# Half of one block's reciprocal loads on ScalarE's queue, two more tiles transposed by DMA, and a new order, in a linear-attention and feed-forward kernel

## The chip, the cores and the metric

The kernel runs on one core of a Trainium2 chip. The metric is the time of one execution on the device, in microseconds (us). The five engines of the core work side by side: TensorE (PE, matmuls; PEld its weight loads), VectorE (DVE), ScalarE (ACT), GpSimd (POOL) and SyncE (SP). Each works through its own instructions in order and waits on semaphores for the others. Transfers are issued by an engine's queue (here SP's, and after the change ScalarE's too) and carried out by DMA engines.

## The reference

A transformer block on 2048 tokens of width 512, in bf16: linear attention with 32 heads of 16, then a feed-forward part of width 1792, each behind a layer norm and with a residual.

```python
x = A_x
h = x + _A_ref(_layernorm(x), A_wqkv, A_wo)
h2 = h + _B_ref(_layernorm(h), B_w1, B_w2)
# _A_ref, on x = layernorm of the input
q, k, v = heads of x @ wqkv
phi = lambda t: jnp.where(t > 0, t + 1, jnp.exp(t)) + 1e-6
pq, pk = phi(q), phi(k)
kv = jnp.einsum("bhsd,bhse->bhde", pk, v)
z = jnp.einsum("bhsd->bhd", pk)
num = jnp.einsum("bhqd,bhde->bhqe", pq, kv)
den = jnp.einsum("bhqd,bhd->bhq", pq, z)[..., None] + 1e-6
return (num / den, heads joined) @ wo
# _B_ref
return maximum(x @ w1, 0) @ w2
```

## The kernel before

The tokens are 16 tiles of 128, in four blocks (c = 0 to 3) of 512. All work is written as words in one list, ORDER (line 18); the loop at line 555 emits them one after the other, and each word is a small function `op_...`. A word such as `K.1.0.0.2` is the function's name and its numbers. The words of one engine run in the order of the list; between engines only the semaphores of true dependences count. So ORDER fixes five queues, and nothing else sets the order. PSUM is one tile `bk` of eight banks, and the last number or so of a word on TensorE is its bank; a word that writes a bank waits until the bank's last reader is done.

The stages, with their words:

- Loads on SP: `lx` (x, in groups of tiles), `lk`, `lq`, `lv`, `lo`, `l1`, `l2` (weights for k, q, v, wo, w1, w2; the last two in halves of 896 KB).
- First layer norm, tile t: `S` (statistics, VectorE), `A` (their sum, VectorE), `R` (inverse root, two instructions on ScalarE), `N` (normalise into `h_nat`, VectorE). Then the transpose into `lnT[c]`: tiles 0 to 4 on TensorE (`T`, four 128x128 transposes against an identity, with the eviction `E` on ScalarE), tiles 5 to 15 by a DMA transpose on SP (`X`, line 308).
- Keys, tile t: `K` (four matmuls of 512 columns, or two halves of two), `F` (exp) and `U` (relu) on ScalarE out of PSUM, `M` (min with 1) and `D` (add) on VectorE into pk. Queries, block c, quarter j: `Q` and likewise `qF`, `qU`, `qM`, `qD` into `pqT[c]`.
- The statistics product `G` of tile t: four matmuls of ln by pk into banks 4 to 7, summed over all 16 tiles (G multiplies by what `D` of the tile wrote). The sums z: `za`, `zf`, `zhi`, `zlo` on VectorE and the short matmuls `z`; `zc`, `zh` on VectorE.
- `gA`, `gD` evict G (ScalarE, VectorE); `kv` multiplies by the v weights, `kx` (VectorE) masks to the heads' blocks, `m` multiplies by wo, `mA` and `mD` evict that.
- The denominators of block c: `d4` (TensorE), `dl4` and `dx4` (ScalarE, ln and exp(-)), `wb` (a store of the reciprocals to a scratch tensor in DRAM, SP), `rb` (line 470: eight loads from it, one for each head position, each spread over 16 partitions of `rr`), `dm` (VectorE: pqT by rr into `pqs`; two instructions of two quarters each). There is one `rr`, so the loads of a block wait for the `dm` of the block before.
- Tile t: `h` (pqs by m, TensorE), `hD` (plus x, VectorE), second norm `s`, `a`, `r`, `n` or `nA` (VectorE or ScalarE), whose transpose is `t` (TensorE, four transposes) with the copy `v` (VectorE), or `x` (DMA transpose on SP, line 309). Tiles 2 and 3 have `t` and `v`, all others `x`.
- Feed-forward: `p` (w1, 512 tokens) or `ph` (256 of them: half 0 is tiles 0 and 1 of the block, half 1 is tiles 2 and 3), evicted in pairs by `pD` (VectorE) or `pA` (ScalarE) with the relu; `f` (w2, tile t, the fourteen slices f in two halves of seven), `fo` (VectorE, scale and residual), `fd` (store, SP).
- `warm` are matmuls on zeros at the start, `masks` and `const` constants.

Two functions of TensorE matter for the change: `op_K` (line 312) and `op_f` (line 533) set start at slice 0 and stop at the last slice, so their halves run in rising order.

Of the kernel before, what the change touches and what calls it, by code (L numbers as in the profile page):

```python
# [34 lines left out]
ph.0.1.3.0 ph.0.2.0.0 ph.0.3.1.1 qM.2.2.2 qM.3.0.2 ph.0.0.2.0 ph.0.0.2.1 qM.3.2.2 qD.3.0.2 qU.3.2.2 qD.2.2.2  # L35
ph.0.2.0.1 qD.3.2.2 p.0.7.5 d4.2.6.2 pD.0.2.2 dl4.2 dl4.3 rb.1.4 rb.1.6 rb.1.3 rb.1.2 rb.1.0 rb.1.1 ph.0.1.3.1
rb.1.7 rb.1.5 p.0.6.4 dx4.2 dm.1.0.2 dm.1.2.2 h.4.0 pD.0.0.2 hD.4 pD.0.6.2 p.0.5.1 h.6.6 dx4.3 p.0.4.0 hD.6
l2.7.7 h.5.4 pA.0.4.2 s.4 s.6 hD.5 h.7.7 a.4 a.6 p.0.11.6 p.0.10.5 s.5 hD.7 a.5 p.0.9.4 wb.2 rb.2.6 n.4 rb.2.0
rb.2.4 s.7 n.6 rb.2.3 rb.2.2 rb.2.1 a.7 n.5 n.7 rb.2.5 rb.2.7 dm.2.0.2 dm.2.2.2 pD.0.10.2 p.0.13.1 p.0.12.0
p.0.8.3 pD.0.12.2 wb.3 r.4.4 rb.3.0 rb.3.4 h.10.7 hD.10 x.6 h.8.2 h.11.6 hD.8 s.10 rb.3.5 rb.3.1 rb.3.6  # L40
f.1.0.0.7 rb.3.3 rb.3.2 rb.3.7 s.8 hD.11 pD.0.8.2 h.9.5 f.3.1.0.7 x.7 x.5 s.11 a.8 hD.9 f.1.0.7.7 f.0.4.0.7 a.10
a.11 x.4 dm.3.2.2 dm.3.0.2 h.14.7 h.12.3 s.9 n.11 h.15.6 a.9 n.10 h.13.2 fo.1 n.9 n.8 hD.14 s.14 hD.12 x.11
hD.15 f.0.4.7.7 r.8.4 p.1.13.7 p.1.6.3 a.14 hD.13 s.12 s.15 s.13 a.12 a.15 a.13 n.14 p.1.12.6 n.13 f.3.1.7.7
n.12 n.15 p.1.2.5 fo.0 pD.1.12.2 x.10 p.1.7.4 fo.3 p.1.3.6 x.9 pD.1.6.2 pD.1.2.2 r.12.4 x.8 p.1.11.2 p.1.10.1
pD.1.10.2 f.2.4.0.7 p.2.0.6 p.2.1.7 f.2.4.7.7 pD.2.0.2 p.2.10.0 p.2.11.1 fo.2 x.14 p.2.6.2 p.2.7.3 x.15 fd.3
p.2.13.7 p.2.12.6 pD.2.10.2 pD.2.6.2 x.12 fd.1 pD.2.12.2 p.2.2.0 x.13 fd.0 p.2.3.1 p.1.5.6 p.1.4.5 pD.2.2.2
pD.1.4.2 p.1.0.3 p.1.1.4 p.1.9.1 p.1.8.0 pD.1.0.2 pD.1.8.2 f.4.4.0.7 f.4.4.7.7 fo.4 fd.4 f.5.3.0.7 f.5.3.7.7
fo.5 fd.2 f.6.7.0.7 f.6.7.7.7 fo.6 p.2.4.2 p.2.5.3 f.7.0.0.7 f.7.0.7.7 pD.2.4.2 fo.7 p.3.6.1 p.3.7.2 pD.3.6.2
# [539 lines left out]
```

## Time and profile before

| | us |
|---|---|
| median of 3 runs | 169.78 |
| lowest and highest | 169.41, 170.17 |
| span of the profiled execution | 168.0 |

The profiled execution's time outside its span is not in the records; the difference of median and span is 1.78 us. The profile's page gives each engine's busy time and share of the span, and the span in 40 slices of 4.2 us with the busy tenths of each engine. The chain of waits goes back from the last instruction to what released it each time. The timeline lists instructions in order of time, like ones merged (x2 are two); its columns are start, length, engine, line, operation, written and read tile, shapes. TensorE's ends are modelled: matmuls overlap, so a single one shows as 0.38 us long.

The memory side: the 16 DMA engines are busy in tenths `4984054681595364414552520000101000011021` over the 40 slices.

### The profile page before, as it was taken

The page shows a single profiled execution, that of the slowest core. Times are in us where ns is not written, and L with a number is a line of the kernel's source. Part 1 is how long each engine was busy: PE and PEld are TensorE (multiplying, and loading weights), DVE is VectorE, ACT ScalarE, POOL GpSimd, SP SyncE. Part 2 cuts the span into 40 slices and gives each one's busy share as a digit, 9 for nine tenths or more (in the row PEclk, how much of TensorE's full clock was granted, in tenths as well). Part 3 has the DMA queues.
Part 4 walks back from the last instruction along what each step waited for, and adds up shares of the span by engine and source line. Part 5 has one row for each costly group of instructions (what it writes and reads, how often), then busy time and mean ns, then how long its engine had stood idle before and what let it go on. Part 6 is the DMA issues. An engine that isn't in the chain of part 4 may idle for free.

```text
span 168.0 us, 2417 instructions
## 1 busy us (share of the span) xinstructions
PE 162.7 (97%) x924; PEld 79.2 (47%) x924; DVE 115.6 (69%) x217; ACT 49.5 (29%) x83; POOL 4.8 (3%) x21
## 2 busy tenths in 40 slices
PE   7799999999999999999999999999999999999992
...
DVE  3899999942579999999999755764144773432312
...
DMA  4984054681595364414552520000101000011021
GB/s 108 353 298 88 20 106 95 189 301 45 132 337 161 98 205 132 132 48 123 83 102 57 126 63 0 0 0 0 62 31 35 0 0 7 32 34 48 31 94 39
DMA packets 25003, 16.01 MB, mean 95 GB/s; under 512 B 15008, under 2 KB 23968, under 8 KB 24992
## 3 DMA queue, kind: packets, MB, share of 16 engines
...
q8 instruction: 7, 0.11, 0.3%
...
## 4 chain that ended last, share of the span: by engine, by line
PE 92%; DMA 4%; SPq 2%; DVE 1%; issue 0%
PE bk L537 28%; PE bk L508 27%; PE bk L324 8%; PE bk L368 8%; PE bk L493 8%; PE bk L316 7%; DMA wq_sb<-in_A_wqkv_dram 4%; PE bk L517 2%; SPq L214 2%; PE bk L440 1%; DVE gT L545 1%; PE bk L392 1%; PE bk L414 1%; PE bk L426 1%; PE bk L287 0%
## 5 line engine op out<-in xcount | busy, mean ns | idle before, releaser
L537 PE MATMUL bk<-w_sb,at 128*128 128x512 bf16 (+2 forms) x252 | 50.0, 355 | 0.0
L508 PE MATMUL bk<-lnT,w_sb 128*128 128x512 bf16 x208 | 46.9, 379 | 0.0
L528 DVE TENSOR_SCALAR at<-bk 128x1024 bf16<-128x1024 f32 x27 | 32.8, 1223 | 13.2 <-PE bk L508 13.2
L537 PEld LDWEIGHTS <-at 128*128 128x128 bf16 x252 | 23.5, 98 | 25.4
L508 PEld LDWEIGHTS <-w_sb 128*128 128x128 bf16 x208 | 20.4, 98 | 23.9
L545 DVE SCALAR_TENSOR_TENSOR gT<-bk,rstd,h_nat 128x512 bf16<-128x512 f32 (+2 forms) x18 | 12.4, 691 | 24.6 <-PE bk L537 22.0
L334 ACT ACTIVATE eb<-bk 128x1024 bf16<-128x1024 f32 (+1 forms) x18 | 16.6, 929 | 5.3 <-PE bk L316 2.8
L337 ACT ACTIVATE rb<-bk 128x1024 bf16<-128x1024 f32 (+1 forms) x18 | 16.4, 929 | 0.0
L324 PE MATMUL bk<-lnT,wq_sb 128*128 128x512 bf16 x64 | 15.1, 379 | 0.3 <-DMA wq_sb<-in_A_wqkv_dram 0.3
L316 PE MATMUL bk<-wk_sb,lnT 128*128 128x512 bf16 x64 | 15.3, 379 | 0.0
L493 PE MATMUL bk<-m_sb,pqs 128*128 128x512 bf16 x64 | 15.1, 379 | 0.0
L368 PE MATMUL bk<-at,h_nat 128*128 128x512 bf16 x56 | 13.1, 379 | 0.0
L248 DVE BATCH_NORM_STATS2 st<-x_nat 128x6 f32<-128x512 bf16 x16 | 10.6, 678 | 2.3 <-DMA x_nat<-in_A_x_dram 2.3
L499 DVE TENSOR_TENSOR h_nat<-bk,x_nat 128x512 bf16<-128x512 f32 x16 | 10.6, 676 | 0.9 <-PE bk L493 0.9
L254 ACT ACTIVATE rstd<-mv,eps 128x2 f32<-128x2 f32 (+2 forms) x14 | 4.2, 297 | 23.7 <-DVE mv L251 20.9
L250 DVE BATCH_NORM_STATS2 st<-h_nat 128x6 f32<-128x512 bf16 x16 | 10.5, 684 | 0.1
L324 PEld LDWEIGHTS <-wq_sb 128*128 128x128 bf16 x64 | 6.1, 98 | 7.7 <-DMA wq_sb<-in_A_wqkv_dram 0.8
L493 PEld LDWEIGHTS <-pqs 128*128 128x128 bf16 x64 | 6.1, 98 | 7.7 <-DVE pqs L484 0.6
L368 PEld LDWEIGHTS <-h_nat 128*128 128x128 bf16 x64 | 6.1, 98 | 7.3 <-issue 0.2
L316 PEld LDWEIGHTS <-lnT 128*128 128x128 bf16 x64 | 6.1, 98 | 6.8
L341 DVE TENSOR_SCALAR eb<-eb 128x1024 bf16<-128x1024 bf16 (+1 forms) x18 | 6.6, 389 | 0.0
L262 DVE TENSOR_SCALAR h_nat<-x_nat,mv,rstd 128x512 bf16<-128x512 bf16 x16 | 6.3, 408 | 0.2 <-ACT rstd L255 0.2
...
## 6 DMA issues: line engine op xcount, KB each, us to landing
...
```

The costliest lines, as they stand in the source:

```text
L248: op_S = lambda t: nc.vector.bn_stats(out=st[:, t, :], in_=x_nat[:, t, :])
L316: nc.tensor.matmul(bk[:, b, :], lhsT=lnT[c][:, kd, j * P : (j + 1) * P], rhs=wk_sb[:, kd, :], start=(kd == 0), stop=(kd == KD - 1),)
L324: nc.tensor.matmul(bk[:, b, :], lhsT=wq_sb[:, kd, j * P : (j + 1) * P], rhs=lnT[c][:, kd, :], start=(kd == 0), stop=(kd == KD - 1),)
L334: nc.scalar.activation(out=buf(eb, kind, i, n), in_=bank(at_bank[kind, i], n), func=ACT.Exp)
L337: nc.scalar.activation(out=buf(rb, kind, i, n), in_=bank(at_bank[kind, i], n), func=ACT.Relu)
L368: nc.tensor.matmul(bk[:, KD + kd, :], lhsT=ln_nat[:, t, kd * P : (kd + 1) * P], rhs=pk(t)[:, 0, :], start=(not stated), stop=(len(stated) ...
L493: nc.tensor.matmul(bk[:, b, :], lhsT=pqs[:, (c * KD + jb) % NQ, j * P : (j + 1) * P], rhs=m_sb[:, jb, :], start=(jb == 0), stop=(jb == KD ...
L499: nc.vector.tensor_tensor(out=h_nat[:, t : t + n, :], in0=bank(at_bank["h", t], n), in1=x_nat[:, t : t + n, :], op=ALU.add,)
L508: nc.tensor.matmul(bk[:, b, :], lhsT=w1_sb[:, kd, f * P : (f + 1) * P], rhs=lnT[c][:, kd, :], start=(kd == 0), stop=(kd == KD - 1),)
L528: nc.vector.tensor_scalar(out=acts[c % 2][:, f : f + n, :], in0=bank(at_bank["p", c, f], n), scalar1=-1.0, scalar2=0.0, op0=ALU.mult, op1= ...
L537: nc.tensor.matmul(bk[:, b, 0 : w * P], lhsT=acts[c % 2][:, f, j * P : (j + 1) * P], rhs=w2_sb[:, f, k * P : (k + w) * P], start=(f == 0), ...
L545: nc.vector.scalar_tensor_tensor(out=o_t[:, t % NO, cols], in0=bk[:, at_bank["f", t, k], 0 : w * P], scalar=rstd2[:, t : t + 1], in1=h_nat ...
```

## The change

Four things change.

1. A new word `ab` is `rb` issued by ScalarE's queue (`spread(nc.scalar, ...)`). In block 0, head positions 1, 3, 5 and 7 are loaded by `ab`, the other four by `rb`; blocks 1 to 3 keep eight `rb`.
2. `t.2`, `v.2`, `t.3`, `v.3` go; `x.2` and `x.3` come in. TensorE has eight transposes fewer, VectorE two copies fewer, SP two DMA transposes more.
3. `part` counts the parts of a K or f sum as they are emitted, so the halves may run in any order; the new order uses this.
4. ORDER is a new permutation of all the other words, with many other banks.

The code:

```diff
+    fed = {}
+
+    def part(key, n):
+        at = fed[key] = fed.get(key, 0) + 1
+        return {"start": at == 1, "stop": at == n}
+
...
                 bk[:, b, :], lhsT=lnT[c][:, kd, j * P : (j + 1) * P], rhs=wk_sb[:, kd, :],
-                start=(kd == 0), stop=(kd == KD - 1),
+                **part(("k", t), KD),
...
-    def op_rb(c, h):
-        nc.sync.dma_start(
+    def spread(eng, c, h):
+        eng.dma_start(
             out=rr[h * DH : (h + 1) * DH, :, :],
             in_=scr[c][:, h, :, :].rearrange("j o n -> o j n").broadcast_to([DH, KD, CW]),
         )
+
+    op_rb = lambda c, h: spread(nc.sync, c, h)
+    op_ab = lambda c, h: spread(nc.scalar, c, h)
...
                 rhs=w2_sb[:, f, k * P : (k + w) * P],
-                start=(f == 0), stop=(f == KF - 1),
+                **part(("f", t, k), KF),
```

The order, up to the first feed-forward products:

```diff
-table const masks warm.70.7.64 warm.2.7 lx.0.1 S.0 A.0 R.0.1 lx.1.1 S.1 lx.2.1 A.1 N.0 T.0.1 lk.0.4 S.2 R.1.1
-N.1 T.1.2 lx.3.1 A.2 E.0 K.0.4 R.2.1 lx.4.2 S.3 N.2 T.2.1 E.1 A.3 S.5 R.3.1 K.1.0.0.2 K.1.0.2.2 N.3 S.4 A.5 A.4
-E.2 T.3.2 K.2.6.0.2 K.2.6.2.2 F.0.1 M.0.1 lx.6.2 E.3 S.7 lq.0.4 R.4.2 lx.8.4 Q.0.3.1 N.4 U.0.1 A.7 F.1.1 F.2.1
-T.4.2 N.5 S.6 Q.0.1.4 U.1.1 M.1.1 A.6 lx.12.4 M.2.1 D.0.1 R.6.2 K.3.7.0.2 K.3.7.2.2 E.4 X.5 U.2.1 U.3.1 D.1.1
-N.6 Q.0.0.3 N.7 S.10 qF.0.0.2 K.4.5 K.5.6 S.8 A.10 S.9 A.8 qU.0.0.2 S.12 F.4.2 D.2.1 X.6 Q.0.2.0 A.9 A.12 K.6.2
-S.13 S.11 M.4.2 A.11 A.13 U.4.2 D.4.2 F.3.1 R.8.2 N.9 M.3.1 X.7 K.7.3 R.12.2 R.10.2 N.8 F.6.2 D.3.1 N.13 S.15
...
-lo.0.2 lo.2.2 zc zh d4.0.1 dl4.0 l1.0.2 G.13 G.12 G.15 dx4.0 gA.2.2 Q.1.1.3 Q.1.0.2 qF.1.0.2 gD.0.2 kv.1.4
-kv.3.4 kv.0.4 kv.2.4 kx qU.1.0.2 qM.1.0.2 qD.1.0.2 Q.1.3.1 Q.1.2.0 qF.1.2.2 m.0.2 m.1.3 mD.0.2 m.3.7 m.2.6 wb.0
-Q.2.0.4 Q.2.1.5 rb.0.7 rb.0.1 rb.0.6 rb.0.3 rb.0.0 rb.0.2 rb.0.4 rb.0.5 l1.2.2 qM.1.2.2 qU.1.2.2 Q.2.3.1
-qD.1.2.2 mA.2.2 qF.2.0.2 Q.2.2.0 qU.2.0.2 dm.0.2.2 dm.0.0.2 qM.2.0.2 h.1.6 hD.1 s.1 a.1 qU.2.2.2 d4.1.3 dl4.1
-h.0.7 hD.0 s.0 dx4.1 h.2.6 h.3.5 a.0 l2.0.7 wb.1 hD.2 nA.1 hD.3 qF.2.2.2 nA.0 s.2 s.3 Q.3.0.2 Q.3.1.3 a.2
-Q.3.3.6 a.3 qF.3.0.2 qU.3.0.2 Q.3.2.5 x.1 r.0.4 qF.3.2.2 n.2 t.2.7 n.3 t.3.4 qD.2.0.2 v.2 v.3 x.0 ph.0.3.1.0
...
+table const lx.0.1 warm.70.7.64 lx.1.1 masks lx.2.1 lk.0.4 lx.3.1 S.0 lx.4.2 S.1 lx.6.2 lq.0.4 A.0 warm.2.7 A.1
+S.2 R.0.1 lx.8.4 R.1.1 N.0 lx.12.4 A.2 N.1 T.0.1 R.2.1 T.1.2 E.0 N.2 E.1 T.2.7 S.3 K.0.1 E.2 A.3 S.4 R.3.1
+K.2.4.0.2 F.0.1 N.3 K.1.6.0.2 S.5 U.0.1 T.3.7 K.1.6.2.2 E.3 A.4 A.5 K.2.4.2.2 S.7 R.4.2 K.3.7.2.2 M.0.1 F.2.1 S.6
+K.3.7.0.2 F.1.1 Q.0.1.3 A.7 N.4 U.1.1 M.1.1 N.5 U.2.1 T.4.1 A.6 Q.0.0.2 S.8 X.5 R.6.2 D.0.1 E.4 Q.0.2.0 A.8 N.6
+U.3.1 D.1.1 X.6 F.3.1 N.7 Q.0.3.1 M.2.1 qF.0.0.2 S.9 K.4.4 X.7 M.3.1 A.9 qU.0.0.2 S.13 K.5.5 S.12 R.8.2 l2.7.7
+S.11 K.6.2 U.4.2 A.12 A.13 D.2.1 K.7.3 A.11 F.4.2 N.8 N.9 X.8 qM.0.0.2 R.12.2 D.3.1 G.0 M.4.2 qF.0.2.2 S.14 X.9
+G.1 S.10 F.6.2 G.3 S.15 U.6.2 N.13 G.2 A.10 A.15 X.13 A.14 N.12 R.10.2 qD.0.0.2 K.8.2 R.14.2 D.4.2 qU.0.2.2 X.12
+K.9.3 M.6.2 N.11 D.6.2 G.5 F.8.2 N.14 K.13.1 N.10 X.14 U.8.2 qM.0.2.2 M.8.2 K.12.0 N.15 za.4.1 X.15 G.4 F.12.2
+D.8.2 G.6 X.10 U.12.2 za.6.0 G.9 X.11 M.12.2 K.14.2 za.8.0 K.15.3 lv.0.2 l1.0.2 zf K.10.0 lv.2.2 F.14.2 D.12.2
+lo.0.2 K.11.1 zhi l2.0.7 U.14.2 qD.0.2.2 G.12 zlo F.10.2 M.14.2 G.7 U.10.2 M.10.2 D.14.2 G.13 D.10.2 G.8 z.0.2
+z.2.2 z.1.2 z.3.2 G.11 zc zh d4.0.1 G.10 dl4.0 dx4.0 G.15 wb.0 G.14 lo.2.2 Q.1.1.3 gA.2.2 gD.0.2 rb.0.6 Q.1.0.2
+ab.0.3 rb.0.2 ab.0.1 rb.0.0 kv.3.1 kv.0.1 ab.0.7 rb.0.4 kv.2.1 kv.1.1 ab.0.5 l1.2.2 Q.2.1.7 kx qF.1.0.2 m.2.4
+m.0.0 qU.1.0.2 m.1.1 qM.1.0.2 m.3.5 mD.0.2 Q.2.0.6 mA.2.2 Q.1.3.2 dm.0.0.2 qU.2.0.2 dm.0.2.2 Q.1.2.1 qD.1.0.2
+h.1.3 qU.1.2.2 h.0.0 hD.1 qF.2.0.2 Q.3.1.5 s.1 qF.1.2.2 hD.0 h.2.7 a.1 s.0 nA.1 Q.3.0.4 a.0 hD.2 x.1 nA.0 h.3.0
+s.2 qU.3.0.2 Q.2.3.3 x.0 a.2 hD.3 qF.3.0.2 n.2 Q.2.2.2 s.3 x.2 Q.3.2.6 a.3 qF.2.2.2 n.3 qM.1.2.2 x.3 qM.2.0.2
+Q.3.3.7 qU.2.2.2 qD.1.2.2 ph.0.0.4.0 qM.3.0.2 qF.3.2.2 qD.2.0.2 ph.0.2.0.0 d4.1.3 r.0.4 ph.0.1.5.0 qM.3.2.2 dl4.1
+qD.3.0.2 ph.0.3.1.0 ph.0.1.5.1 qM.2.2.2 dx4.1 ph.0.0.4.1 qU.3.2.2 wb.1 p.0.8.3 pD.0.0.2 ph.0.3.1.1 ph.0.2.0.1
...
```

The rest of the list, from there to the end, is permuted as well: the p, f and h words of blocks 0 to 3 come in another order and other banks. At the end the last full tile is 12 in both, and the last 128 columns of tile 15 follow it.

More of the change, by code (lines that the diff above doesn't have):

```diff
@@ L34 @@
-Q.3.3.6 a.3 qF.3.0.2 qU.3.0.2 Q.3.2.5 x.1 r.0.4 qF.3.2.2 n.2 t.2.7 n.3 t.3.4 qD.2.0.2 v.2 v.3 x.0 ph.0.3.1.0
[L35 to L48, printed above, removed]
```

27 lines of the change are left out of this document (18 added, 9 removed).

## The prediction

> **What bounds the kernel now.** I read the page first, then the chain of waits in order of time, then the timeline of the stretches in which the order changes.
>
> ```profile
> span 168.0 us, 2417 instructions
> PE 162.7 (97%) x924; PEld 79.2 (47%) x924; DVE 115.6 (69%) x217; ACT 49.5 (29%) x83; POOL 4.8 (3%) x21
> ...
> PE   7799999999999999999999999999999999999992
> ...
> DVE  3899999942579999999999755764144773432312
> ```
>
> TensorE is busy in every slice but the first two and the last. VectorE reads 9 or nearly so in slices 2 to 8 and again in 13 to 22: there it has little to give, and a late VectorE result would show up on TensorE.
>
> ```profile
> 4.16 6.17 DMA wq_sb<-in_A_wqkv_dram
> ...
> 10.38 1.04 PE bk L324 x4
> ...
> 18.54 5.18 PE bk L368 x24
> ...
> 37.67 0.33 PE bk L440 x4
> ...
> 49.36 0.86 PE bk L493 x4
> ...
> 56.70 0.45 PE bk L287 x8
> 57.15 3.06 PE bk L517 x28
> ...
> 144.54 19.66 PE bk L537 x91
> ```
>
> In each line: start, length, what. The chain (the view named last: start and length in us) reaches TensorE at 10.38, when the query weights have landed, and stays on it until 164.20 (144.54 + 19.66). One 512-column matmul takes 5.18/24 = 0.216 us there, a block of four 0.86; a half-width one takes 3.06/28 = 0.109. So the time is the head up to 10.38, a fixed queue of matmuls, and the tail after the last full tile. A change gains only by an earlier head or by fewer matmuls, and loses by each new hole. The kernel's median is 169.78, the span 168.0; I make the sum on the span and carry the 1.78 between them unchanged.
>
> **Part 1, two tiles transposed by DMA.** The eight TensorE transposes of t.2 and t.3 go: the row at 56.70 gives 0.45 us, all of it on the chain. VectorE loses the two copies v.2 and v.3. In their place come two DMA transposes on SP, and the first half-products on tiles 2 and 3 must not come before they land.
>
> ```profile
> 53.34 1.25 DVE L499 TENSOR_TENSOR h_nat<-bk,x_nat 128x512 bf16<-128x512 f32 x2
> ...
> 54.51 1.28 DVE L250 BATCH_NORM_STATS2 st<-h_nat 128x6 f32<-128x512 bf16 x2
> ...
> 55.92 0.60 DVE L270 TENSOR_SCALAR hn<-h_nat,mv 128x512 bf16<-128x512 bf16 x2
> ```
>
> ```profile
> L308 SPq DMA_TRANSPOSE lnT<-h_nat x11: 1189/1217/1831, 11.1 to 28.6; - x11
> ...
> DMA to landing us min/median/max: 2.4/2.4/3.4
> ```
>
> After h.3 VectorE does hD.3, n.2, s.3, a.3, n.3: about 0.6 + 0.3 + 0.6 + 0.1 + 0.35 = 2.0 us; then x.3 needs 0.25 until SP has issued x.2 (1.2 each) and 2.4 to land: 4.6 us. TensorE has, between the end of h.3 and ph.0.1.5.1, four query blocks (3.45), four half blocks (16 matmuls of half width, 0.44 a block, 1.75) and d4.1 (0.33): 5.5 us. That cover of 0.9 us hides the two DMAs; with the longest landing (3.4) nothing is over and 0 to 0.1 us is paid. SP issues wb.1 behind x.3, but wb.1 waits for dx4.1 some 3 us longer anyway. I take 0.45 gained, bounds 0.35 and 0.45.
>
> **Part 2, the head.** The loads keep their order on SP, so x and the weights land as now. What changes is the order on VectorE, ScalarE and TensorE.
>
> ```profile
> 5.09 0.40 PE L287 MATMUL bk<-ident,h_nat 128*128 128x128 bf16 x4
> ...
> 6.14 0.29 ACT L254 ACTIVATE rstd<-mv,eps 128x1 f32<-128x1 f32 x1
> ...
> 6.47 0.20 ACT L255 ACTIVATE rstd<-rstd 128x1 f32<-128x1 f32 x1
> 6.58 0.58 ACT L297 ACTIVATE lnT<-bk 128x512 bf16<-128x512 bf16 x1
> 6.62 0.69 DVE L248 BATCH_NORM_STATS2 st<-x_nat 128x6 f32<-128x512 bf16 x1 [0.51 <-DMA x_nat<-in_A_x_dram]
> 7.23 0.40 DVE L262 TENSOR_SCALAR h_nat<-x_nat,mv,rstd 128x512 bf16<-128x512 bf16 x1
> ...
> 11.10 1.83 SPq L308 DMA_TRANSPOSE lnT<-h_nat  x1
> ```
>
> Now N.2 (7.23) stands behind S.3, which waits for x until 6.62. In the new order N.2 comes first. S.1 ahead of A.0 makes T.0 later, 5.49 instead of 5.09; then N.1 ends at 5.9 and N.2, one square-root pair (0.53) later, runs from 6.15 to 6.55, so T.2 starts at 6.60 and its eviction E.2 (0.58, from 7.03) ends at 7.6. K.0 runs from 6.82, the halves of K.2 and K.1 up to 8.54; N.3 (after S.3, and R.3 which stands behind E.2) ends at 8.50, T.3 runs 8.56 to 8.78, the other halves to 9.64, E.3 ends at 9.57 and K.3 runs to 10.50. There wq has been in place since 10.33 (4.16 + 6.17). So Q.0.1 starts at 10.50 with four K blocks done, where now a query block starts at 10.38 with three: 0.86 - 0.12 = 0.74 us ahead. The links E.2 to K.2 and E.3 to K.3 hold by less than 0.1 us; if both fail by 0.2, 0.34 stays.
>
> **Part 3, whether the lead lasts to the statistics product.** The rest of the DMA transposes X follow VectorE's N. X.5 is now issued at 11.10, as N.5 ends; in the new order S.6 and M.1 (0.6 and 0.2 by the rows below) stand before N.5, and it ends at 11.6. X.5 then lands before 15.0 (11.6 + 3.4), K.5 is due at 15.03. X.6 is issued at 13.1, X.7 at 14.35, K.7 due at 16.8 = 14.35 + 2.4. So G.0 starts about 17.7 instead of 18.54, at a lead of 0.8 less 0.05. From there VectorE decides.
>
> ```profile
> 13.36 1.28 DVE L248 BATCH_NORM_STATS2 st<-x_nat 128x6 f32<-128x512 bf16 x2
> ...
> 19.50 0.41 DVE L262 TENSOR_SCALAR h_nat<-x_nat,mv,rstd 128x512 bf16<-128x512 bf16 x1
> 19.82 0.42 DVE L344 TENSOR_TENSOR at<-rb,eb 128x512 bf16<-128x512 bf16 x1
> ...
> 25.02 0.69 DVE L344 TENSOR_TENSOR at<-rb,eb 128x1024 bf16<-128x1024 bf16 x1
> 25.62 1.22 DVE L376 TENSOR_TENSOR zacc<-at 128x1024 f32<-128x1024 bf16 x1
> 26.76 0.42 DVE L341 TENSOR_SCALAR eb<-eb 128x1024 bf16<-128x1024 bf16 x1
> 27.09 1.23 DVE L376 TENSOR_TENSOR zacc<-zacc,at 128x1024 f32<-128x1024 f32 x1
> ```
>
> From start to start an instruction takes less than its length: 0.60 for a statistic, 0.32 for N, 0.34 for a 512-wide add, 0.60 for a 1024-wide add, 1.14 for za, 0.33 for a 1024-wide M, 0.2 for a narrow M, 0.08 for an A. Behind N.7 (its slot ends at 13.64) stand, up to D.8.2: seven statistics 4.2, eight N 2.56, two narrow M 0.4, two narrow D 0.68, five wide M 1.65, three wide D 1.8, za.4 1.14, some eight A 0.6: 13.0 us. So D.8.2 starts at 26.65 and ends at 27.34. G.9 multiplies by it. TensorE, dense from 17.72, has eleven blocks before G.9 and gets there at 27.22: a hole of about 0.2. The transposes in this stretch hold: X.13, X.12, X.14 land 0.3, 0.0 and 0.9 us before their K by the same sums, and l2.7.7, whose 896 KB now go out between X.7 and X.8, is taken below. The lead is 0.75 - 0.15 = 0.6 at the z sums; VectorE late by half a microsecond more leaves 0.1, VectorE early leaves 0.75.
>
> **Part 4, the reciprocals' loads on two queues.**
>
> ```profile
> 40.73 1.02 ACT L406 ACTIVATE gT<-bk 128x1024 bf16<-128x1024 f32 x1 [1.33 <-PE bk L368]
> ...
> 41.17 0.80 SPq L471 DMA_DIRECT2D rr<-scr  x2
> ...
> 43.35 0.69 DVE L422 TENSOR_TENSOR kvbd<-bk,mask 128x512 bf16<-128x512 f32 x1 [1.82 <-PE bk L414]
> ...
> 45.51 1.23 DVE L432 CAST m_sb<-bk 128x1024 bf16<-128x1024 f32 x1 [0.34 <-PE bk L426]
> ...
> 47.78 1.29 DVE L484 TENSOR_TENSOR pqs<-pqT,rr 128x1024 bf16<-128x1024 bf16 x2
> ```
>
> ```profile
> L471 SPq DMA_DIRECT2D rr<-scr x32: 303/424/529, 41.2 to 77.8; - x32
> ...
> DMA to landing us min/median/max: 2.2/2.6/3.0
> ```
>
> Times here are in the old frame; the lead moves all of them alike. Eight issues from 41.17, at 0.45 each, end at 44.8, and the last lands near 47.0. With four on ScalarE, behind gA (ends 41.75), the last is issued at 43.15 and lands at 45.75 to 46.15. The new order needs them earlier: h.1 stands eight matmuls (1.73 us) earlier behind d4.0, near 47.65, and the second dm must end by 47.9, so the first must start by 46.7. That fits by 0.5 us. ScalarE pays four issues, for which the trace has no row on that engine: SP's 0.30 and 0.53 are the bounds, I take 0.45, 1.8 in all. Behind them on ScalarE stand qF.1.0, qU.1.0 and mA; qF ends near 44.6, qU at 45.5, and Q.1.3, which wants their bank, is due near 45.95: hidden, with 0.1 still over at 0.53 an issue. On SP only lo.2.2 moves in between wb.0 and the loads; it is issued while SP waits for wb.0.
>
> One wait is new. Now two query blocks (1.73) cover the masking kx (0.69) before the m products; afterwards one block (0.86). kx ends 0.72 after the last kv product, a dependent matmul starts 0.06 to 0.13 after its releaser (5.09 above came 0.06 after N.0), and the group's first matmul starts about 0.16 before the chain's mark: 0.15 us lost, bounds 0 and 0.2.
>
> **The rest** (c = 1 to 3 and the tail): same matmuls, pairs of p blocks (1.73) over one pD of 1.2 us. I followed each bank and each half sum f to its releaser: the tightest are h.7 behind dm.1 (0.4 us) and f.14's second half behind pD.3.12 (0.45). The tail again is f.12, then fo.12, the last 128 columns of tile 15, and their two stores. Nothing is taken.
>
> **Sum:** 0.45 + 0.6 - 0.15 = 0.90 us; span 167.1, time 168.88, 0.5% under the median. I call 0.5% what this kernel's measurement can tell from no change (168.93 and 170.63).
>
> **Rivals.**
>
> *The head's lead is lost in the X and D chain.* For it: sums of a dozen instructions with margins of 0.1; VectorE's 9s there. Against: VectorE does the same work as now. Then only 0.45 less 0.15 stays: 169.5. That the two queues do nothing for the reciprocals, since the landing bounds them, ends there too: with the last landing at 47.0 the second dm would end at 48.3 for 47.9, 0.4 of the 0.9 lost, 169.3.
>
> *X.8 waits behind l2.7.7.* The weights' load moves from late in the kernel to between X.7 and X.8.
>
> ```profile
> L220 SPq DMA_DIRECT2D w_sb<-in_B_w_dram x4: 427/447/468, 32.0 to 59.4; - x4
> ...
> DMA to landing us min/median/max: 5.1/6.2/7.1
> ```
>
> It is issued at about 15.6 and lands between 20.7 and 22.7; X.8, issued at 17.5, lands at 19.9 to 20.9 if loads in flight don't hold it, and K.8 is due at 21.2. For it: X.5, the one transpose issued while loads were under way, took the 3.4. Against: nothing else loads at that time, so 5.1 is the nearest row. If the transpose comes 0.6 behind a load that takes 7.1, X.8 lands at 23.3, K.8 waits 2.1, and with the 0.2 at G.9 swallowed the time is 168.88 + 1.9 = 170.8: slower. It decides from a landing of X.8 later than 22.1, where the whole 0.9 is gone. The Trainium skill, "DMA: Bandwidth & Descriptors", section "Queues, rings and completion order", says that each DMA engine takes the descriptors of a queue in ring order; by that rule X.8 can't land before the weights have been read, at any load. The 3.4 of X.5 agrees, and no row of before shows a transpose behind weights of this size.
>
> **Chances.** Forecast 0.56, lost lead 0.17, weights ahead of X.8 (with whatever else is late by two microseconds) 0.27. The forecast's own range is 168.4 to 169.3, of which 0.40 lies below 168.93 and 0.16 above. Lost lead counts as no change, the third as slower. Faster 0.40, same 0.33, slower 0.27. The range goes from 168.3 (no hole at G.9 nor behind kx: 0.45 + 0.75 is 1.2, a little more with a better landing of X) to 170.8, the second rival.
>
> **What would show it.** Right: no TensorE transposes behind the fourth h block, and a chain that goes from the last Q to ph without a wait; Q.0.1 near 10.5 with four K blocks before it; G.0 near 17.7; G.9 held shortly by VectorE's add; rr landed before mD ends. Wrong: TensorE idle on lnT in 15 to 31, a wait for pqs at h.1, ScalarE's issues longer than 0.5, or idle time in the later p and f blocks, where I took none.

## The result: slower by 0.7%

| | before | changed |
|---|---|---|
| median of 12 runs each, side by side | 169.85 | 170.73 |
| lowest and highest | 169.15, 170.17 | 170.27, 171.97 |
| span of the profiled execution | 168.0 | 169.3 |

The ratio is 1.0068, 95% interval 1.0051 to 1.0085. The forecast was 168.88, so the sign was wrong; the time lies inside the range, at its upper end, where the second rival had put it (170.8).

The profile after, from its page:

```profile
span 169.3 us, 2384 instructions
...
PE   7899989999999999999999999999999999999992
...
DVE  3899999943489968674999989616366588010552
...
PE 83%; DVE 8%; DMA 5%; SPq 1%; issue 1%
```

TensorE has an 8 in slice 6 (21 to 25 us), where it had 9. TensorE now makes up 83% of the chain that ended last, 92% before: VectorE's work on the first layer norm, a DMA that ends at 22.57 and some VectorE work near 88 us have come into it.

Where the time went is read by setting the starts of the same stages beside each other. First the timeline of TensorE before (start, length, engine, line, operation, tiles; idle time before it and its releaser in brackets). A few matmul records are missing, so a count can be short:

```profile
18.38 1.89 PE L368 MATMUL bk<-pk_lo,h_nat 128*128 128x512 bf16 x8
...
37.60 0.40 PE L440 MATMUL bk<-pqT,zhd 128*32 128x512 bf16 x4
...
44.88 1.03 PE L426 MATMUL bk<-wo_sb,kvbd 128*128 128x512 bf16 x4
...
53.09 3.62 PE L324 MATMUL bk<-lnT,wq_sb 128*128 128x512 bf16 x16
...
56.99 3.22 PE L517 MATMUL bk<-lnT,w_sb 128*128 128x256 bf16 x28
```

and the same view of the changed kernel:

```profile
10.81 1.03 PE L330 MATMUL bk<-lnT,wq_sb 128*128 128x512 bf16 x4
...
14.49 3.67 PE L322 MATMUL bk<-wk_sb,lnT 128*128 128x512 bf16 x16
18.41 1.89 PE L374 MATMUL bk<-pk_lo,h_nat 128*128 128x512 bf16 x8 [0.24 <-ACT eb L340]
20.13 1.89 PE L374 MATMUL bk<-at,h_nat 128*128 128x512 bf16 x8
22.62 1.69 PE L322 MATMUL bk<-wk_sb,lnT 128*128 128x512 bf16 x7 [0.59 <-DMA lnT<-h_nat]
...
38.40 0.40 PE L446 MATMUL bk<-pqT,zhd 128*32 128x512 bf16 x4
...
43.95 1.03 PE L330 MATMUL bk<-lnT,wq_sb 128*128 128x512 bf16 x4
44.97 1.04 PE L432 MATMUL bk<-wo_sb,kvbd 128*128 128x512 bf16 x3
...
53.62 3.62 PE L330 MATMUL bk<-lnT,wq_sb 128*128 128x512 bf16 x15
57.07 1.04 PE L526 MATMUL bk<-lnT,w_sb 128*128 128x256 bf16 x8
...
87.77 0.59 PE L502 MATMUL bk<-m_sb,pqs 128*128 128x512 bf16 x2
88.75 2.33 PE L502 MATMUL bk<-m_sb,pqs 128*128 128x512 bf16 x10 [0.39 <-DVE pqs L493]
```

Read the differences:

- **Head.** The first query block comes at 10.81 with four K blocks done; before at 10.38 with three (0.86 less work). That is 0.43 ahead.
- **G.0.** Four K blocks run dense from 14.49, 16 × 0.2156 = 3.45, to 17.94. G.0 starts at 18.41: a hole of 0.47, and the lead is gone (18.38 before).
- **K.8.** Two G pairs from 18.41 end at 21.86. K.8 starts at 22.62: a hole of 0.75. At d4.0 the changed kernel is 0.80 behind (38.40 against 37.60).
- **kx.** One query block from 43.95 ends at 44.81, m starts at 44.97: 0.16.
- **Transposes.** The last four query blocks start 0.53 late (53.62 against 53.09), the half-products only 0.08 late (57.07 against 56.99): 0.45 won.
- **h.14.** Its last two matmuls wait for pqs: from 87.77 two matmuls run to 88.20, the others start at 88.75: 0.55.

The sum is −0.43 + 0.47 + 0.75 + 0.16 − 0.45 + 0.55 = +1.05. VectorE's last outputs, that of the last full tile and of the last 128 columns, show the same; first before, then changed:

```profile
164.22 1.13 DVE L545 SCALAR_TENSOR_TENSOR gT<-bk,rstd,h_nat 128x512 bf16<-128x512 f32 x2 [2.27 <-PE bk L537]
```

```profile
165.30 1.13 DVE L554 SCALAR_TENSOR_TENSOR gT<-bk,rstd,h_nat 128x512 bf16<-128x512 f32 x2 [0.76 <-PE bk L546]
```

They are 1.08 later. From there to the end of the span it is 4.0 after and 3.8 before, which makes up the 1.3 by which the span grew.

**What ends the three holes.** The chain of waits of the changed kernel (start, length, what) has the one at K.8:

```profile
17.36 0.33 DVE h_nat L268 x2
17.69 4.88 DMA lnT<-h_nat
...
22.62 1.47 PE bk L322 x6
```

and SP's timeline has the load that stands ahead of X.8:

```profile
15.90 0.57 SPq L226 DMA_DIRECT2D w_sb<-in_B_w_dram  x1
```

X.8 is issued at 17.69, right behind N.8 and N.9, and lands 4.88 us later; X.5 to X.7 of before were down after 2.4 to 3.4. l2.7.7, issued at 15.90, lands at 21.29, and X.8 lands 1.28 behind it. For h.14, VectorE's and SP's timelines of the changed kernel, then one row of ScalarE's:

```profile
68.65 1.28 DVE L493 TENSOR_TENSOR pqs<-pqT,rr 128x1024 bf16<-128x1024 bf16 x2
...
78.39 1.29 DVE L493 TENSOR_TENSOR pqs<-pqT,rr 128x1024 bf16<-128x1024 bf16 x2 [3.11 <-DMA rr<-scr]
...
88.03 0.66 DVE L493 TENSOR_TENSOR pqs<-pqT,rr 128x1024 bf16<-128x1024 bf16 x1
```

```profile
68.10 2.56 SPq L474 DMA_DIRECT2D scr<-rd  x2
70.84 11.52 SPq L477 DMA_DIRECT2D rr<-scr  x14
```

```profile
69.68 0.62 ACT L457 ACTIVATE rd<-ld 128x512 bf16<-128x512 f32 x1
```

wb.2 and wb.3 stand one behind the other on SP (the row at 68.10), and the reads rb.2 behind both. wb.3 needs dx4.3, which ScalarE runs behind the ReLU pA.0.4 (68.76 to 69.78) at 69.68 to 70.30; SP stands until then before it issues wb.3, and rb.2 starts at 70.84. dm.2 stands in VectorE's order and waits 3.11 us. VectorE then catches up for ten microseconds, and dm.3 ends at 88.69, too late for h.14. The hole at G.0 is a bank: G.0 to G.3 write banks 4 to 7, and F.4 (ScalarE, 17.34 to 18.36) still reads 4 and 5:

```profile
17.34 1.02 ACT L340 ACTIVATE eb<-bk 128x1024 bf16<-128x1024 f32 x1
```

### The profile page after: what moved, and what is told of

The parts are those of the page before. It is cut to its first block, busy times and chain, and to the rows that moved or that the text cites. A ratio compares the mean times of both kernels' runs of the same rounds, so it can differ in the third digit from the quotient of the medians.

```text
span 169.3 us, 2384 instructions
## 1 busy us (share of the span) xinstructions
PE 162.1 (96%) x900; PEld 78.6 (46%) x916; DVE 114.7 (68%) x215; ACT 49.7 (29%) x83; POOL 4.8 (3%) x21
## 4 chain that ended last, share of the span: by engine, by line
PE 83%; DVE 8%; DMA 5%; SPq 1%; issue 1%
PE bk L546 28%; PE bk L517 26%; PE bk L502 8%; PE bk L374 6%; PE bk L330 6%; PE bk L322 4%; DVE st L254 4%; DMA lnT<-h_nat 3%; DMA x_nat<-in_A_x_dram 2%; PE bk L526 2%; DVE h_nat L268 1%; SPq L220 1%; PE bk L446 1%; DVE pqs L493 1%; DVE mv L255 1%
## 5 line engine op out<-in xcount | busy, mean ns | idle before, releaser
L517 PE MATMUL bk<-lnT,w_sb 128*128 128x512 bf16 x203 | 46.1, 379 | 0.2
L537 DVE TENSOR_SCALAR at<-bk 128x1024 bf16<-128x1024 f32 x27 | 32.1, 1218 | 10.9 <-PE bk L517 9.7
L502 PE MATMUL bk<-m_sb,pqs 128*128 128x512 bf16 x64 | 15.8, 379 | 0.4 <-DVE pqs L493 0.4
L322 PE MATMUL bk<-wk_sb,lnT 128*128 128x512 bf16 x63 | 14.8, 379 | 0.6 <-DMA lnT<-h_nat 0.6
L493 DVE TENSOR_TENSOR pqs<-pqT,rr 128x1024 bf16<-128x1024 bf16 x8 | 5.2, 683 | 3.5 <-DMA rr<-scr 3.5
```

The lines of the kernel that those rows point to most:

```text
L322: nc.tensor.matmul(bk[:, b, :], lhsT=lnT[c][:, kd, j * P : (j + 1) * P], rhs=wk_sb[:, kd, :], **part(("k", t), KD),)
L502: nc.tensor.matmul(bk[:, b, :], lhsT=pqs[:, (c * KD + jb) % NQ, j * P : (j + 1) * P], rhs=m_sb[:, jb, :], start=(jb == 0), stop=(jb == KD ...
L517: nc.tensor.matmul(bk[:, b, :], lhsT=w1_sb[:, kd, f * P : (f + 1) * P], rhs=lnT[c][:, kd, :], start=(kd == 0), stop=(kd == KD - 1),)
L537: nc.vector.tensor_scalar(out=acts[c % 2][:, f : f + n, :], in0=bank(at_bank["p", c, f], n), scalar1=-1.0, scalar2=0.0, op0=ALU.mult, op1= ...
```

## The experiments

All of them change the order of the changed kernel, unless another base is named. Ratios are to the kernel before, run beside them; its medians were 169.64 (first four), 169.60 (next four) and 169.49 (last three).

**1. The weights behind X.8.**

```diff
-S.9 K.4.4 X.7 M.3.1 A.9 qU.0.0.2 S.13 K.5.5 S.12 R.8.2 l2.7.7
+S.9 K.4.4 X.7 M.3.1 A.9 qU.0.0.2 S.13 K.5.5 S.12 R.8.2
...
-kv.2.1 kv.1.1 ab.0.5 l1.2.2 Q.2.1.7 kx
+kv.2.1 kv.1.1 ab.0.5 l1.2.2 l2.7.7 Q.2.1.7 kx
```

> The changed kernel with one load moved: l2.7.7 (896 KB) goes from between X.7 and X.8 to behind l1.2.2. Theory (the ninth tile's transpose waits for the weights that were put ahead of it): X.8 lands about 2.4 us after its issue instead of 4.9, K.8 starts at about 21.9 instead of 22.6, without a wait; 0.7 us of the loss goes, and the time is about 0.2% over the kernel before (170.1 us). Rival (VectorE's N.8 is what is late, the load does not matter): X.8 still lands after 22, and the time stays about 0.7% over.

Measured: 170.31 (169.65 to 171.01), ratio 1.0040 (1.0018 to 1.0062). Of the 0.7 us expected the two ratios show 0.28%, 0.47 us. K.8 does not wait for X.8 any more: it is issued at 18.3 and lands 3.4 later, not the 2.4 expected, but in time. But the x group of tile 8 came late in this execution, and S.8, which stands ahead of N.6 in the new order, held the line. The chain, then TensorE's timeline:

```profile
4.64 7.89 DMA x_nat<-in_A_x_dram
...
12.55 0.69 DVE st L252
```

```profile
16.48 1.04 PE L320 MATMUL bk<-wk_sb,lnT 128*128 128x512 bf16 x4 [0.43 <-DMA lnT<-h_nat]
17.76 1.04 PE L320 MATMUL bk<-wk_sb,lnT 128*128 128x512 bf16 x4 [0.24 <-DMA lnT<-h_nat]
```

So the cause of the 0.75 at K.8 is shown, and a second exposure: the new order puts a statistic whose data comes late ahead of the normalisations that feed X.6 and X.7.

**2. The bank of G.0 alone.** Q.0.2.0 goes between K.5 and K.6, R.8 behind F.4, N.8 and N.9 behind M.4 (X.8 behind them), so that F.4 is done before G.0.

```diff
-Q.0.2.0 A.8 N.6 U.3.1 ... K.5.5 S.12 R.8.2 ... F.4.2 N.8 N.9 X.8 ... G.0 M.4.2
+A.8 N.6 U.3.1 ... K.5.5 Q.0.2.0 S.12 ... F.4.2 R.8.2 ... G.0 M.4.2 N.8 N.9 X.8
```

> The changed kernel with the hole ahead of G.0 taken away and the weights left where they are: Q.0.2 runs between K.5 and K.6, R.8 behind F.4, N.8 and N.9 behind M.4. Theory (G.0 waits for F.4 to empty bank 4; what follows is set by the landing of X.8 anyway): G.0 starts at about 18.0 instead of 18.4, the hole ahead of K.8 grows by as much, K.8 stays at 22.6 or comes some tenths later because N.8 is later; time within 0.3 us of the changed kernel, about 0.7% over the kernel before. Rival (the two holes add independently): 0.4 us faster than the changed kernel, 0.45% over the kernel before.

Measured: 171.14 (170.66 to 171.69, 6 runs), ratio 1.0084 (1.0057 to 1.0112). G.0 has no wait for a bank, and nothing is won: K.8 still waits for X.8, and the query block that is now third waits 0.27 for another bank (E.4). In this execution S.3 waited for x until 7.46 (6.87 in the changed kernel), and the whole head was later by that; that nothing is won is read from the medians.

**3. wb.3 behind rb.2.**

```diff
-p.0.13.5 dx4.3 h.7.3 wb.3 rb.2.2 h.4.2 ... rb.2.5 s.4 rb.2.4 f.3.2.7.7
+p.0.13.5 dx4.3 h.7.3 rb.2.2 h.4.2 ... rb.2.5 s.4 rb.2.4 wb.3 f.3.2.7.7
```

> The changed kernel with the store wb.3 moved behind the eight loads rb.2. Theory (h.14 waits for dm.3, dm.3 for a VectorE that stood 3.1 us at dm.2, and dm.2 for loads that SP could issue only after wb.3, which waits for dx4.3): the loads start 0.8 us earlier, dm.2 starts at 77.5 or earlier instead of 78.4, the wait of h.14 of about 0.55 us goes, the time is about 0.35% over the kernel before. Rival (VectorE's work between dm.2 and dm.3, not its start, sets dm.3): the hole at h.14 stays and the time too.

Measured: 170.57 (170.19 to 171.63), ratio 1.0067 (1.0044 to 1.0090): the time alone shows nothing, and the 0.35% expected lies outside the interval. The stages of the profiled execution do: K.8 is at 22.80, 0.18 later than in the changed kernel, and VectorE's last outputs are at 164.93, 0.37 earlier, so 0.55 is won in between. TensorE has no wait for pqs, and dm.2 waits 0.85 in place of 3.11 (the profile names the store as the releaser, but wb.3 lands only at 78.03; the last of the loads lands at 76.04). VectorE and SP:

```profile
76.31 1.29 DVE L491 TENSOR_TENSOR pqs<-pqT,rr 128x1024 bf16<-128x1024 bf16 x2 [0.85 <-DMA scr<-rd]
```

```profile
70.15 3.58 SPq L475 DMA_DIRECT2D rr<-scr  x8
74.26 0.35 SPq L472 DMA_DIRECT2D scr<-rd  x1
78.17 3.58 SPq L475 DMA_DIRECT2D rr<-scr  x8
```

All eight rb.2 are out at 73.73, ahead of the store; in the changed kernel at 74.73. That is 1.0, and dm.2 starts 2.1 earlier: the longest landing of these loads fell from 3.9 to 2.8 as well; why it fell is not shown. The stretch from d4.0 to VectorE's last outputs tells how firm the size is. It takes 126.34 to 126.46 in the runs with the store behind and the same order otherwise (3, 4, 5, 10), and with it ahead 126.90 in the changed kernel, 126.55 in experiments 1 and 8, 126.81 in 2. In these the last of the eight loads lands 39.60 after d4.0 (changed kernel), 39.26 (1 and 8) and 39.51 (2), and the stretch follows it one for one. So the store ahead costs 0.1 to 0.55, by how late the last load lands.

**4. The three edits together** (1, 2 and 3).

```diff
-K.5.5 S.12 R.8.2 l2.7.7 ... F.4.2 N.8 N.9 X.8 ... h.7.3 wb.3 rb.2.2
+K.5.5 Q.0.2.0 S.12 ... F.4.2 R.8.2 ... M.4.2 N.8 N.9 X.8 ... l1.2.2 l2.7.7 ... h.7.3 rb.2.2
```

> All three moves in the changed kernel. Theory (the three holes of about 0.45, 0.75 and 0.55 us are the whole of the loss, and the removed transposes and the earlier head remain): span about 167.6, time about 0.5% to 0.6% under the kernel before. Rival (new holes further on, VectorE's chain to D.8 or the loads of block 2, take half of it): time within 0.2% of the kernel before.

Measured: 169.69 (169.50 to 171.17), ratio 1.0014 (0.9988 to 1.0040): level with the kernel before. The 0.5% to 0.6% of the theory did not come; the time is the rival's. G.0 is at 18.45, K.8 at 21.91 without a wait, h.14 has none. One new hole remains, the bank of experiment 2:

```profile
13.28 1.02 PE L328 MATMUL bk<-lnT,wq_sb 128*128 128x512 bf16 x4 [0.27 <-ACT lnT L301]
```

**5. More moves.** As 4 (with R.8, N.8 and N.9 where it has them), but Q.0.3 in place of Q.0.2 between K.5 and K.6, the statistic S.8 behind N.7 with A.8 behind S.9, and the store fd.14 ahead of fd.9.

```diff
-Q.0.0.2 S.8 X.5 ... Q.0.2.0 A.8 N.6 ... N.7 Q.0.3.1 M.2.1 qF.0.0.2 S.9 K.4.4 ... K.5.5 S.12 ... fd.9 fd.14
+Q.0.0.2 X.5 ... Q.0.2.0 N.6 ... N.7 M.2.1 S.8 qF.0.0.2 S.9 A.8 K.4.4 ... K.5.5 Q.0.3.1 S.12 ... fd.14 fd.9
```

> The changed kernel with the weights' load later and wb.3 behind rb.2 as before, and the head mended in another way: Q.0.3 (instead of Q.0.2) between K.5 and K.6, so that no query block waits for the eviction of T.4; R.8 behind F.4, N.8 and N.9 behind M.4; S.8, which can wait for its load, behind N.7; and the store of tile 14 ahead of that of tile 9 at the end. Theory (the loss is the sum of the named holes): G.0 starts near 18.0, K.8 without a wait, z near 35.3, no wait at h.14, the stretch from the last VectorE instruction to the end 0.2 us shorter; span about 167.2, time 0.3% to 0.6% under the kernel before. Rival (the lead is taken back by VectorE's chain to D.8, or by x landing late): z at 35.7 as in the kernel with three moves, time equal to the kernel before.

Measured: 170.14 (169.58 to 170.98), ratio 1.0026 (1.0005 to 1.0047). The rival held: with N.8 later, X.8 is issued at 19.48, and K.9 waits 0.29 for X.9; x of tile 3 came at 7.07, and all but 0.1 of the lead at the first query block was gone (11.13). The move of the store changed nothing that can be seen.

**6. One queue for the reciprocals** (the four `ab.0` are `rb.0` again, in the same places).

```diff
-rb.0.6 Q.1.0.2 ab.0.3 rb.0.2 ab.0.1 rb.0.0 kv.3.1 kv.0.1 ab.0.7 rb.0.4 kv.2.1 kv.1.1 ab.0.5
+rb.0.6 Q.1.0.2 rb.0.3 rb.0.2 rb.0.1 rb.0.0 kv.3.1 kv.0.1 rb.0.7 rb.0.4 kv.2.1 kv.1.1 rb.0.5
```

> The changed kernel with all eight reciprocal loads of block 0 on SP's queue. Theory (the new order needs the loads 1.7 us earlier and the second queue pays for that): the last load is issued near 45.4 instead of 43.9, rr is there near 48.0 instead of 47.4, dm.0 starts there, h.1 waits 0.4 to 0.6 us, time 0.3% above the changed kernel. Rival (the loads are bound by landing, which got longer with two queues, 3.2 to 3.4 us against 2.6): rr at 47.4 to 47.6 and no difference.

Measured: 171.42 (171.28 to 171.83, 4 runs), ratio 1.0114 (1.0085 to 1.0143). Changed kernel first (VectorE, and the group of ScalarE's issues: count, shortest, median and longest in ns, first and last start), then this one (TensorE and VectorE):

```profile
47.41 1.29 DVE L493 TENSOR_TENSOR pqs<-pqT,rr 128x1024 bf16<-128x1024 bf16 x2 [0.35 <-DMA rr<-scr]
```

```profile
L477 ACTq DMA_DIRECT2D rr<-scr x4: 309/402/439, 42.0 to 43.5; - x4
```

```profile
48.77 2.07 PE L500 MATMUL bk<-m_sb,pqs 128*128 128x512 bf16 x8 [0.35 <-DVE pqs L491]
```

```profile
48.02 1.29 DVE L491 TENSOR_TENSOR pqs<-pqT,rr 128x1024 bf16<-128x1024 bf16 x2 [1.15 <-DMA rr<-scr]
```

dm.0 waits 1.15 for the loads in place of 0.35, and TensorE, done with its query blocks at 48.26, stands 0.51 at h.1. The rival's premise holds: the eight landed in 2.9 to 3.5 us on two queues, in 2.5 to 2.7 on one. But the last of them was issued 1.55 behind the first on two queues and 3.31 on one, which is more than the longer landing took back. Half the loads on a second queue are worth this half microsecond in the new order, and only because that order needs them earlier; in the old one h.1 didn't wait.

**7. The transposes' time put back** (eight 128-column matmuls without a use ahead of ph.0.1.5.1, on the kernel of experiment 5).

```diff
-ph.0.3.1.0 ph.0.1.5.1
+ph.0.3.1.0 warm.8.2.128 ph.0.1.5.1
```

> The kernel with all moves, and eight matmuls of 128 columns on zeros ahead of ph.0.1.5.1, as many and as wide as the transposes that the change took away, with nobody waiting for them. Theory (TensorE is dense there, so each matmul costs its slot): everything behind is 0.45 us later, time 0.27% above the kernel with all moves. Rival (slack behind takes it up): less than 0.15 us.

Measured: 170.46 (170.22 to 171.07), ratio 1.0054 (1.0034 to 1.0073) against 1.0026 for experiment 5: 0.28%, 0.47 us, with intervals of 0.2% on either side. On TensorE:

```profile
58.65 0.61 PE L249 MATMUL bk<-m_sb 128*128 128x128 bf16 x8
59.09 1.04 PE L524 MATMUL bk<-lnT,w_sb 128*128 128x256 bf16 x8
```

From start to start the eight take 0.44, and from d4.0 to the last outputs it takes 126.78, 0.32 more than in experiment 5 and 0.44 more than in 4 and 10. The transposes cost their whole place, and the 0.45 won by taking them out is real.

**8. Twice the weights ahead of X.8** (l2.0.7 moved to just behind l2.7.7).

```diff
-S.12 R.8.2 l2.7.7
+S.12 R.8.2 l2.7.7 l2.0.7
```

> The changed kernel with the other half of w2 (l2.0.7, 896 KB) put behind l2.7.7, so that 1.8 MB instead of 0.9 MB stand ahead of X.8. Theory (the transpose waits until the loads ahead of it in the queue are through): X.8 lands 2.5 to 3 us later, near 25.3, the wait at K.8 grows from 0.75 to about 3.4 us, the time by 2 us or more. Rival (the transposes only share the bandwidth with one load): X.8 lands at most 1 us later.

Measured: 174.79 (173.17 to 175.47, 4 runs), ratio 1.0295 (1.0248 to 1.0341). The chain and TensorE's timeline:

```profile
18.20 7.55 DMA lnT<-h_nat
```

```profile
25.80 3.57 PE L320 MATMUL bk<-wk_sb,lnT 128*128 128x512 bf16 x8 [3.26 <-DMA lnT<-h_nat]
```

A further 896 KB ahead of X.8 puts its landing from 22.57 to 25.75. The landing follows what has been queued before it: 2.4 to 3.4 without a load (experiments 5 and 1), 4.88 behind one, 7.55 behind two. In the profiled execution, the slowest of the four, the later landing makes 3.2 at K.8 against the changed kernel. A further 1.65 is TensorE's clock: after the wait the eight matmuls at 25.80 take 3.38 from start to start in place of 1.73, and the granted clock in 26 to 30 us is 0.60, while it is 1.0 in the changed kernel behind its shorter wait.

The Trainium skill, "DMA: Bandwidth & Descriptors", section "Queues, rings and completion order", has each DMA engine consume the descriptors of an issuing engine's queue in ring order. These landings agree with it.

**9. The transposes by DMA in the old order.** Base: the kernel before. x.2 and x.3 replace t.2, t.3, v.2, v.3; x.0 goes up to x.1, and one half-product up.

```diff
-x.1 r.0.4 qF.3.2.2 n.2 t.2.7 n.3 t.3.4 qD.2.0.2 v.2 v.3 x.0 ph.0.3.1.0
-ph.0.1.3.0 ph.0.2.0.0 ph.0.3.1.1 qM.2.2.2 qM.3.0.2 ph.0.0.2.0
+x.1 x.0 r.0.4 qF.3.2.2 n.2 x.2 n.3 x.3 qD.2.0.2 ph.0.3.1.0
+ph.0.1.3.0 ph.0.2.0.0 ph.0.0.2.0 ph.0.3.1.1 qM.2.2.2 qM.3.0.2
```

> The old order with one part of the change alone: tiles 2 and 3 of the first 512 tokens transposed by DMA (x.2, x.3 behind n.2, n.3; the eight TensorE transposes and the copies v.2, v.3 gone), and one half-product moved so that four of them, as in the changed kernel, stand ahead of the first that needs tiles 2 and 3. Theory (by the stages of the two traces the transposes give 0.45 and only the new order loses): 0.45 us under before, 169.2 for a before of 169.65, the first half-product 0.45 earlier behind the last query block and no wait of it for lnT. Rival (the DMA transposes have a price of their own, landing late beside wb.1 and l2.0.7, which is issued near them in the old order): TensorE waits for lnT ahead of the half-products, 169.6 to 170.2.

Measured: 173.13 (172.74 to 173.50, 5 runs), ratio 1.0185 (1.0133 to 1.0238). Both theories missed, by far: the rival had the right kind of wait, not its size. TensorE, then SP:

```profile
59.79 1.48 PE L524 MATMUL bk<-lnT,w_sb 128*128 128x256 bf16 x12 [1.40 <-DMA lnT<-hn]
...
65.55 1.21 PE L500 MATMUL bk<-m_sb,pqs 128*128 128x512 bf16 x4 [1.47 <-DVE pqs L491]
```

```profile
52.42 6.11 SPq L313 DMA_TRANSPOSE lnT<-hn  x4
58.62 3.81 SPq L475 DMA_DIRECT2D rr<-scr  x8
```

There are two prices, and a small third, 0.37 at h.14 behind dm.3. x.3 is issued at 57.3 and lands 2.4 later, behind the half-products that were to cover it. And rb.1, which follows on SP, starts at 58.62; in the kernel before it started at 55.58. dm.1 waits 2.3 for it, and h.4, which the old order has two p blocks behind the half-products, stands 1.47. So the transposes by DMA are no gain by themselves. The new order makes them one: there SP is done with x.3 at 57.5, wb.1 can't go before 60.1 anyway, and h.7, the first of its block, stands far behind.

**10. The new order without any bank moved** (edits 1 and 3, and S.8 and A.8 as in 5).

```diff
-Q.0.0.2 S.8 X.5 ... Q.0.2.0 A.8 N.6 ... M.2.1 qF.0.0.2 S.9 ... R.8.2 l2.7.7 ... h.7.3 wb.3 rb.2.2
+Q.0.0.2 X.5 ... Q.0.2.0 N.6 ... M.2.1 S.8 qF.0.0.2 S.9 A.8 ... R.8.2 ... l1.2.2 l2.7.7 ... h.7.3 rb.2.2
```

> The changed kernel with l2.7.7 behind l1.2.2 (past X.8), wb.3 behind rb.2, and the statistic S.8 behind N.7, A.8 behind S.9; no bank is moved. Theory (0.75 at K.8 and 0.55 at h.14 are these two edits; the 0.47 at G.0 stays): 1.3 us under the changed kernel, 169.4 for 170.7, no wait for lnT at K.8 and none for pqs at h.14; G.0 near 18.4 still with its wait for eb. Rival (whatever is won is taken again by the next late statistic, as in the run with all moves): K.8 or K.9 waits 0.3 to 0.6 for lnT, 169.9 to 170.2.

Measured: 169.69 (169.52 to 170.50), ratio 1.0006 (0.9982 to 1.0031); the changed kernel had 1.0068. Of the theory's 1.3 us the two ratios give 0.62%, 1.05 us; the profiled span, 167.9, is 1.4 shorter than that of the changed kernel. TensorE, and VectorE's last outputs:

```profile
18.24 1.89 PE L372 MATMUL bk<-pk_lo,h_nat 128*128 128x512 bf16 x8 [0.24 <-ACT eb L338]
19.96 1.89 PE L372 MATMUL bk<-at,h_nat 128*128 128x512 bf16 x8
21.89 1.89 PE L320 MATMUL bk<-wk_sb,lnT 128*128 128x512 bf16 x8
```

```profile
164.00 1.13 DVE L552 SCALAR_TENSOR_TENSOR gT<-bk,rstd,h_nat 128x512 bf16<-128x512 f32 x2 [0.76 <-PE bk L544]
```

G.0 still waits for its bank; K.8 and h.14 wait for nothing that the list of waits shows (0.2 is lost at K.8, where U.6, the last reader of its bank, ends at 21.84), and from d4.0 to the last outputs it takes 126.34, where the kernel before takes 126.62.

**11. Old order to z, new order behind it** (with wb.3 behind rb.2). Base: the list of the kernel before as far as z.1.0, then that of experiment 3, with the G words, lo.0.2, l1.0.2, l2.0.7 and l2.7.7 that would be missing at the seam put in.

```diff
 ... z.0.0 z.2.0 z.3.0 z.1.0
-G.14 lo.0.2 lo.2.2 zc zh d4.0.1 dl4.0 l1.0.2 G.13 G.12 G.15 dx4.0 gA.2.2 Q.1.1.3 Q.1.0.2 ...
+G.14 zc zh d4.0.1 G.13 dl4.0 G.12 dx4.0 G.15 wb.0 lo.2.2 Q.1.1.3 gA.2.2 gD.0.2 rb.0.6 Q.1.0.2 ab.0.3 ...
```

> The old order up to the z sums, the new one behind them (with the reciprocals' loads on two queues, the transposes by DMA and wb.3 behind rb.2); the G products left over at that place are G.14, G.13, G.12 and G.15 in place of G.11, G.10, G.15 and G.14, and the loads l2.7.7 and l2.0.7 go behind l1.2.2 and behind x.3. Theory (the loss is made ahead of z, 0.79, and at h.14, 0.55): z at 35.65 as before, from there 0.45 won at the transposes and 0.16 lost at kx; with the tail 0 to 0.2 longer 169.4 to 169.6 for a before of 169.7. Rival (behind z the new order loses by something else than wb.3): 170 or more.

Measured: 169.47 (168.99 to 170.32), ratio 0.9990 (0.9967 to 1.0013). The z sums start at 35.50, 0.15 before those of the old kernel, the last outputs at 163.96, 0.26 earlier. Of the 0.29 expected behind z that is 0.11; a hole of 0.13 at h.7 (the tightest place that the prediction had named) takes about the rest. It comes from an edit of this experiment: l2.0.7 now stands ahead of wb.1 on SP and lands at 62.33; wb.1 lands 3.49 after its issue in place of 1.74 in experiment 10, the loads rb.1 start behind that, and dm.1 waits 0.75. The tail from the last outputs to the end of the span is 3.9 against 3.8. This version is the fastest of all, by 0.02 us against the kernel before: no difference. No version beats the kernel before.

## Why the prediction was wrong

**Right by mechanism and size.** The transposes: 0.45 taken, 0.45 measured in the stages, 0.44 when put back (experiment 7). The wait at kx: 0.15 taken, 0.16 measured. ScalarE's four issues: 1.8 in all taken, 1.99 measured (0.40 for the median one, with pauses between), but from 41.99 on, while gA still runs, and not behind it. The two queues: dm.0 waited 0.35 for rr and TensorE felt nothing of it; with one queue it lost 0.51, where the rival had said 0.4 of the lead. The 0.15 taken for G.9 was not paid: TensorE waits for nothing there, neither in the changed kernel nor in experiment 10.

**The step that failed first: "X.8, issued at 17.5, lands at 19.9 to 20.9 if loads in flight don't hold it".** They held it: X.8 was issued at 17.69 and landed at 22.57, past the 22.1 that the prediction had named as the point where the whole gain is gone. The 0.75 at K.8 is the hole of the second rival, which had a chance of 0.27, and experiments 1, 8 and 10 show its cause. "Nothing else loads at that time" was true and kept the load short (l2.7.7 took 5.39, where 5.1 was the nearest row), but it is no argument for the transpose: that lands behind the load on the same queue, so even at 5.1 it would have been no earlier than 20.7, and it came 1.28 after the load. The one row that spoke for the rival, X.5 with 3.4, was weak: X.8 took 3.4 in experiment 1 with no load ahead of it.

That the rival's 170.8 is met to 0.1 is luck. It counted a wait of 2.1 at K.8; there it was 0.75, and the holes at G.0 and h.14, which it did not have, made up the rest.

**The second: "So G.0 starts about 17.7", with X as the only limit.** The prediction says of the rest of the kernel that each bank was followed; here it followed only lnT and VectorE. G.0 needs the banks of K.4 and K.5, and these are free when F.4 ends. In the kernel before the last reader of these two, there U.4, ended at 18.03, and TensorE came to G.0 at 18.38; now F.4 ends at 18.36 and TensorE is there at 17.94. Experiment 2 takes the wait away and wins nothing while X.8 is late. Whether the 0.47 can be won at all is not shown: experiment 4, without this wait, is no faster than 10, which has it (1.0014 and 1.0006).

**The third, a size: the lead of the head, 0.74.** It was 0.43. Four K blocks were done, as predicted, but x of tile 3 came at 6.87 in this execution and at 6.62 in that of before, and N.3, T.3 and K.3 hang on it directly in the new order. In the experiments it came anywhere between 6.50 and 7.46. The new order passes that on: 6.55 gives the first query block at 10.49 (experiment 1), 7.46 gives it at 11.40 (experiment 2). In the old order the first query block does not follow it: 10.38 with x at 6.62, where it waits for the query weights, and 10.13 with x at 6.86 (experiment 9).

**The fourth: "The rest … Nothing is taken."** It went through h.7 and f.14, and not through dm.2. The place was to be found from the trace of before: SP takes its issues in order, wb.3 waits for dx4.3, and the new list puts dx4.3 behind pA.0.4 on ScalarE, which waits for p blocks; a ScalarE activation of that size takes 1.02 in the rows of before. Experiment 3 shows the loss as that one store, standing ahead of eight loads on which VectorE waits: 0.55 in the profiled execution, 0.1 to 0.55 over the kernels that have it there.

**And one that was not a step:** the two DMAs x.2 and x.3 were priced by whether they land in time, and by wb.1 behind them on SP. In the new order that holds. Experiment 9 shows that the same edit in the old order costs 3.6 us, since there rb.1 stands behind them and is due at once. That the gain belonged to the order and not to the edit couldn't be read in the prediction.

**Taken together.** With the two faults of the order mended, and S.8 moved (experiment 10), what is left is −0.29 (−0.45 + 0.16) behind z and +0.06 ahead of it (z at 35.71 against 35.65); the last outputs come 0.22 earlier and the span ends 0.1 earlier. The change as an idea is worth two tenths of a microsecond, which the measurement can't tell from nothing. **Open:** the 0.1 to 0.2 by which the tail behind the last outputs is longer. Experiment 5 moved one store there without effect. It is not the new order: the tail is 3.9 to 4.0 in all twelve profiles of the changed source, also in experiment 9, which ends with the old order, and 3.8 in the one profile of the kernel before.
